# Moving the grad loads to another queue, storing dx in whole tiles and taking two softmax products to the vector engine, in a window-attention backward kernel

## The chip, the cores and the metric

The kernel runs on one core of a Trainium2 chip. The core has a matrix engine (PE; its weight loads are shown apart as PEld), a vector engine (DVE), a scalar engine (ACT), a general engine (POOL) and a synchronisation engine (SP) that computes nothing. SP, ACT and POOL can each issue memory transfers (DMAs) on a queue of their own; 16 transfer engines carry out what all queues hold. Each engine takes its instructions in order and waits on semaphores. Matrix results land in PSUM, eight banks of 128 rows by 512 floats; ACT and DVE copy them from there to the on-chip memory SBUF (128 rows, too).

The metric is the device time of one execution in microseconds (us), the median of several runs. Before the change it is 1978.06 us, the median of three (1970.09, 1978.06, 1981.67).

## The reference

Forward and backward pass of attention in 8 x 8 windows of an image of 256 x 256 pixels with 384 channels, in bf16. The kernel returns the output and the three gradients.

```python
xw = (windows of x)                          # 1024 windows, 64 pixels, C = 384
q, k, v = split(xw @ wqkv)
p = softmax(q @ k.T * C ** -0.5)
o = p @ v @ wo
# and jax.vjp of it with grad_out: gradients of x (out_1), wqkv (out_2) and wo (out_3)
```

## The kernel before

The image is cut into 128 groups of eight windows ("n", `NQ`): four tiles t of two windows each, so that a tile has 128 rows, 64 for each window (w = 0 and 1), and 384 columns. The weights are multiplied together ahead (`A_sb`, `B_sb` and their transposes). One call of `step(n)` (L352) handles group n, and prepares the next ones in its gaps: the projections of group A = n + 3, the softmax of group S = n + 2, transposes of group n + 4, loads of group n + 5.

The order on each engine is as written (`manual_schedule`, L440); waits are put in where two instructions touch the same data, and a transfer from POOL's queue also waits for the transfer eight before it on that queue. Buffers turn round by group number: X 13 groups, DO (the incoming gradient) 5, XT 3, DOT, YHT, YH, OS and DXS 2 each.

In a step, in the order of PE:

- `md` (L198): 48 small products of TT and X, which I use as the mark where a step starts (PS<-TT,X), copied to MD by DVE and ACT.
- a third of the weight-gradient sums of an earlier set of groups (`Block`, L280), in banks 3 and 4; DVE adds the banks to ACC (`add`, L306). Only in steps 0 to 2 there is none waiting (the branch `early`).
- `attn2` (L259), twice: products of the softmax with X, DO and YH; copied to VW.
- `dxs` (L268): the rest of dx into PSUM banks 5 to 7, where `attn` has begun to sum it (`DXB`, L249). Tile t lies at columns 384 t from there on. So bank 5 holds tiles 0 and 1 alone, bank 6 both pairs, bank 7 tiles 2 and 3. `dxs_ev` (L273) has ACT copy a pair of tiles (h = 0, then 1) to DXS, and POOL store it.
- `scores(S)` (L137) into bank 4; `chain0`, `chain2` and `chain3` (L152 to L171) are the softmax of S and its gradient: maximum and difference on DVE (SS), exponential on ACT (PEX), and from there DVE to L169; the last two products (UM and PB, L170 and L171) on POOL.
- `proj(A, 0)` (L119): products of A_sb and XT into banks 0 to 2, copied to YHT by ACT; `outs` (L211): products of B_sb and MD into banks 5 and 6, then 0 and 1, copied to OS by ACT, stored by POOL (`outs_st`, L218); `proj(A, 1)`: of BT_sb and DOT, into banks 7, 2, 4 and 3, copied to YHT by ACT and, the last quarter, by DVE.

The turning transfers are SP's. Each turns a 128 x 1536 bf16 array: X to XT and DO to DOT (`turn_in`, L110) and the two halves of YHT to YH (`turn_yh`, L115). SP's order in step n is: XT of n + 4, DOT of n + 4, the four loads of DO of n + 5 (`load_do`, L106; before L397), two turns YH of S. A turn to YH must have read YHT before `proj` of two groups later is copied into the same buffer.

POOL's order in step n is: loads of X of n + 5 (`load_x`, L102), stores of dx for h = 0 and then h = 1, UM and PB, stores of the output. In PSUM the two windows of a tile of dx stand with their halves exchanged (`attn`, o against r); the store puts that right: for each tile two stores of 64 rows, each from the other half of DXS.

Of the kernel before, what the change touches and what calls it, by code (L numbers as in the profile page):

```python
# [9 lines left out]
ALU = mybir.AluOpType  # L10
# [6 lines left out]
def kernel(  # L17
# [12 lines left out]
    _, H, W, C = x.shape  # L30
# [5 lines left out]
    NQ = (H // 16) * NQC  # L36
# [15 lines left out]
    PE, DVE, ACT, POOL, SP = nc.tensor, nc.vector, nc.scalar, nc.gpsimd, nc.sync  # L52
# [4 lines left out]
    PSF = PS[:].rearrange("p b c -> p (b c)")  # L57
# [12 lines left out]
    DXS = sb.tile([P, 2, 4, C], BF16, name="DXS")  # L70
    SS = sb.tile([P, 4, 64], F32, name="SS")
    PEX = sb.tile([P, 4, 64], F32, name="PEX")
    TM = sb.tile([P, 4, 64], F32, name="TM")
    UM = sb.tile([P, 4, 64], F32, name="UM")
# [13 lines left out]
    def ev(eng, out, in_):  # L88
        if eng is ACT:
            ACT.copy(out=out, in_=in_)  # L90
        else:
            DVE.tensor_copy(out=out, in_=in_)  # L92

    def img(ap, n, t):
        r0, c0 = 16 * (n // NQC), 32 * (n % NQC) + 8 * t
        return ap[0, r0:r0 + 16, c0:c0 + 8, :]

    def bcast(col):
        return ST[:, col, :].unsqueeze(2).to_broadcast([P, 4, 64])


    def load_x(q, n):  # L102
        for t in range(4):
            q.dma_start(out=X[:, (n % NX) * 4 + t, :], in_=img(x, n, t))  # L104

    def load_do(q, n):  # L106
        for t in range(4):
            q.dma_start(out=DO[:, (n % ND) * 4 + t, :], in_=img(grad_out, n, t))

    def turn_in(n, a):  # L110
        src = (X[:, (n % NX) * 4:(n % NX) * 4 + 4, :] if a == 0 else DO[:, (n % ND) * 4:(n % ND) * 4 + 4, :])
        SP.dma_start_transpose(out=XT[:, n % NXT, :, :] if a == 0 else DOT[:, n % NDT, :, :],
                               in_=src.rearrange("p t c -> p (t c)"))
# [5 lines left out]
    def proj(n, a, banks, engs):  # L119
        wgt = A_sb if a == 0 else BT_sb  # L120
        src = (XT[:, n % NXT] if a == 0 else DOT[:, n % NDT]).rearrange("p (t m) k -> p m t k", m=CK)
        i = 0
        for mo in range(CK):
            for t0, t1 in ((0, 4),) if mo < CK - 1 or len(banks) == CK else ((0, 2), (2, 4)):
                o = PS[:, banks[i], 0:P * (t1 - t0)]
                for m in range(CK):
                    mm(o.rearrange("p (t k) -> p t k", k=P), wgt[:, m, mo * P:(mo + 1) * P], src[:, m, t0:t1, :],
                       m == 0, m == CK - 1)
                ev(engs[i], YHT[:, n % NYH, a, mo, P * t0:P * t1], o)
                i += 1  # L130

    def stack(n, a, m0, m1):

        dst = HYS[:, 4 * m0:4 * m1, 0::3, :] if a == 0 else HYS[:, 4 * m0:4 * m1, 1:3, :]
        DVE.tensor_copy(out=dst, in_=YHT[:, n % NYH, a, m0:m1, :].rearrange("p m (t w k) -> p (m t) w k", w=2, k=64))
# [11 lines left out]
    HALF = (slice(0, 64), slice(64, 128))  # L147

    def sd(r, w):
        return PS[HALF[r], 4, w * 256:w * 256 + 256].rearrange("p (t k) -> p t k", t=4)  # L150
# [11 lines left out]
    def chain3(n):  # L162
        pb = PB[:, n % 2]
        DVE.tensor_reduce(out=ST[:, 1, :], in_=PEX[:], axis=AX.X, op=ALU.add)
        DVE.reciprocal(out=ST[:, 2, :], in_=ST[:, 1, :])
        DVE.tensor_tensor(out=pb[:, 1], in0=PEX[:], in1=bcast(2), op=ALU.mult)  # L166
        for w in range(2):
            DVE.tensor_tensor(out=TM[HALF[w]], in0=sd(1 - w, w), in1=pb[HALF[w], 1], op=ALU.mult)  # L168
        DVE.tensor_reduce(out=ST[:, 3, :], in_=TM[:], axis=AX.X, op=ALU.add)  # L169
        POOL.tensor_tensor(out=UM[:], in0=pb[:, 1], in1=bcast(3), op=ALU.mult)  # L170
        POOL.tensor_tensor(out=pb[:, 0], in0=TM[:], in1=UM[:], op=ALU.subtract)  # L171

    def turn_p(n):
        bb = PS[:, 7, 256:512].bitcast(BF16)
        for t in range(4):
            for a in range(2):
                for w in range(2):
                    r = slice(64 * w, 64 * w + 64)
                    o = t * P + a * 64
                    PE.transpose(bb[r, o:o + 64], PB[r, n % 2, a, t, :], ident[r, r])  # L180
        DVE.tensor_copy(out=TT[:, n % 2, :, :, :].rearrange("p t a k -> p (t a k)"), in_=bb)
# [16 lines left out]
    def md(n):  # L198
        for m in reversed(range(CK)):
            for t in range(4):  # L200
                for hh in range(2):
                    for w in range(2):
                        r = slice(64 * w, 64 * w + 64)
                        mm(PS[64 * hh:64 * hh + 64, MB[m][w], t * P:t * P + P],
                           X[r, (n % NX) * 4 + t, m * P + hh * 64:m * P + hh * 64 + 64],
                           TT[r, n % 2, t, :, :], True, True)
            for w in range(2):
                dst = MD[:, m, :, 1:3, :] if w == 0 else MD[:, m, :, 0::3, :]
                ev(DVE if (w == 0) == (m > 0) else ACT, dst, PS[:, MB[m][w], :].rearrange("p (t a k) -> p t a k", t=4, a=2))
# [39 lines left out]
    DXB = 5 * 512  # L249

    def attn_vw(n, t, f):

        attn(n, t, 0, f, DXB + t * C)
        attn(n, t, 1, f + C, DXB + t * C)

    def vw_ev(n, t, f, eng):
        ev(eng, VW[:, (n % NVW) * 4 + t, :, :].rearrange("p a c -> p (a c)"), PSF[:, f:f + 2 * C])
# [13 lines left out]
                lambda c0, c1: AT_sb[:, m, c0:c1], False, m == CK - 1)  # L271

    def dxs_ev(n, h, eng):  # L273
        ev(eng, DXS[:, n % 2, 2 * h:2 * h + 2, :].rearrange("p a c -> p (a c)"),
           PSF[:, DXB + 2 * h * C:DXB + 2 * h * C + 2 * C])
        for t in (2 * h, 2 * h + 1):
            for w in range(2):
                POOL.dma_start(out=img(out_1, n, t)[8 * w:8 * w + 8], in_=DXS[64 * (1 - w):64 * (1 - w) + 64, n % 2, t, :])  # L278

    class Block:  # L280

# [70 lines left out]
    def step(n):  # L352
        S, A = n + 2, n + 3
        doS, doA = S < NQ, A < NQ
        early = not todo
        if n + 4 < NQ:
            turn_in(n + 4, 0)
            turn_in(n + 4, 1)

        md(n)  # L360
        if early:
            if doA:
                proj(A, 0, (3, 4, 0, 5), (ACT, ACT, ACT, DVE))
            if n + 1 < NQ:
                turn_p(n + 1)
            attn_vw(n, 0, 0)
            vw_ev(n, 0, 0, ACT)
            attn_vw(n, 1, 2 * 512)
            attn_vw(n, 2, 2 * 512 + 2 * C)
            vw_ev(n, 1, 2 * 512, DVE)  # L370
            vw_ev(n, 2, 2 * 512 + 2 * C, ACT)
            attn_vw(n, 3, 0)
            vw_ev(n, 3, 0, ACT)
            if doS:
                stack(S, 0, 0, 3)
                stack(S, 1, 0, 3)
            if n + 5 < NQ:
                load_x(POOL, n + 5)
        else:
            blk = todo.pop(0)  # L380
            nb = len(blk.tiles)
            i1, i2 = (7, 15) if nb == 4 * GQ else (nb // 2, nb)
            blk.mms((3, 4), 0, i1)
            attn2(n, 0, (ACT, ACT))
            if doS:
                stack(S, 0, 0, 3)
            if n + 1 < NQ:
                turn_p(n + 1)
            if doS:
                stack(S, 1, 0, 3)  # L390
            blk.mms((3, 4), i1, i2)
            blk.add(4)
            if n + 5 < NQ:
                load_x(POOL, n + 5)
            attn2(n, 1, (ACT, DVE))
        ready(n)
        if n + 5 < NQ:  # L397
            load_do(SP, n + 5)
        if doS:
            turn_yh(S, 0)  # L400
            turn_yh(S, 1)

        dxs(n, 0)
        dxs(n, 1)
        if not early:
            if doS:
                scores(S)
                chain0(S)
            dxs_ev(n, 0, ACT)
            blk.mms((3,), i2, nb)  # L410
        dxs(n, 3)
        dxs(n, 2)
        if early:
            dxs_ev(n, 0, ACT)
            if doS:
                scores(S)
                chain0(S)
        if doS:
            chain2(S)
        dxs_ev(n, 1, ACT)  # L420
        if doS:
            chain3(S)
        if not early:
            blk.add(3)
        if doA:
            proj(A, int(early), (0, 1, 2), (ACT, ACT, ACT))
        else:
            fill(0, 1, 2)
        outs(n, 0, (5, 6), ACT)
        outs(n, 2, (4, 7) if early else (0, 1), ACT)  # L430
        outs_st(n)
        if not early and doA:
            proj(A, 1, (7, 2, 4, 3), (ACT, ACT, ACT, DVE))
        elif not doA:
            fill(7, 2, 4)
# [153 lines left out]
```

## Time and profile before

| | us |
|---|---|
| median of three runs | 1978.06 |
| lowest and highest | 1970.09, 1981.67 |
| the profiled execution | 1985.92 |
| its span on the core | 1983.8 |
| PE busy in it | 1944.9 |
| ACT busy | 1337.1 |
| POOL busy | 1317.0 |
| DVE busy | 1254.8 |

The profile is of one execution; the profiled one took 2.1 us more than its span. A line of groups reads: source line, engine, operation, what is written <- what is read, shapes, how many, then the busy time in us, the mean of one in ns, and the idle time of the engine before them with what ended it. A line of the timeline reads: start in us from the span's start, duration, engine, line, operation, how many were merged, and in brackets the idle time before it and what ended it. SP computes nothing and has no busy time; "SPq" is what its sequencer does, and the duration there is the time that an issue takes SP. "PEclk" is the share of full clock that PE was granted.

### The profile page before, as it was taken

The numbers are of one execution on the slowest core, as the hardware profiler recorded it, in microseconds if no ns is written. First come the engines' busy times: TensorE is split into PE (matmuls) and PEld (weight loads), VectorE is DVE, ScalarE is ACT, GpSimd is POOL, SyncE is SP. The second block draws the span as 40 slices with busy tenths as digits, with TensorE's granted clock in tenths as the row PEclk, the third lists the DMA queues.
The fourth block names the chain that finished last, engine by engine and source line by source line (L and its number), as shares of the span: only waits on it lengthen the run. The fifth ranks groups of instructions, "written<-read, shape, count | busy, mean of one in ns | idle before, by whom it ended". The sixth has DMA issues, their size and how long they took to land.

```text
span 1983.8 us, 78482 instructions
## 1 busy us (share of the span) xinstructions
PE 1944.9 (98%) x32789; PEld 1364.7 (69%) x32789; DVE 1254.8 (63%) x2595; ACT 1337.1 (67%) x2204; POOL 1317.0 (66%) x2315
## 2 busy tenths in 40 slices
PE   8899999999999999999999999999999999999999
PEld 5566776677667666767766776676677677666766
DVE  5665666666666666666666666666666666656664
ACT  5766766666666676667666766766776766667664
POOL 4766766666666667667667666666766766667653
PEclk9999999999999999999999999999999999999999
DMA  9999999999999999999999999999999999999992
GB/s 215 208 204 212 219 208 207 216 208 200 212 214 212 210 200 210 216 209 216 216 212 210 222 212 196 222 206 210 207 224 205 211 208 218 205 199 222 217 165 68
DMA packets 972260, 409.24 MB, mean 206 GB/s; under 512 B 855296, under 2 KB 947264, under 8 KB 971904
## 3 DMA queue, kind: packets, MB, share of 16 engines
q1 hardware_dynamic: 871632, 251.17, 83.5%
q0 software_dynamic: 98496, 151.78, 30.0%
q8 instruction: 256, 4.19, 0.9%
q10 hardware_dynamic: 1776, 1.28, 0.2%
q14 instruction: 100, 0.82, 0.1%
HBM read 101.84 MB, written 101.84 MB: 103 GB/s over the span
## 4 chain that ended last, share of the span: by engine, by line
PE 85%; DMA 10%; ACT 2%; DVE 1%; issue 1%; POOL 0%; ACTq 0%; DVEq 0%; POOLq 0%
PE PS L86 84%; DMA YH<-YHT 10%; PE PS L180 1%; ACT YHT L90 1%; DMA out_dram<-OS 0%; ACT VW L90 0%; DMA X<-in_x_dram 0%; DVE TM L168 0%; POOL out_dram L278 0%; DVE SS L156 0%; DVE ST L154 0%; ACT DXS L90 0%; ACT VW L526 0%; ACT OS L90 0%; DVE PB L166 0%
## 5 line engine op out<-in xcount | busy, mean ns | idle before, releaser
L278 POOL DMA_DIRECT2D out_dram<-DXS x1024 | 578.0, 571 | 570.5 <-ACT DXS L90 512.2
L86 PE MATMUL PS<-VW,X 64*64 64x384 bf16 (+1 forms) x8661 | 578.1, 325 | 0.0
L86 PEld LDWEIGHTS <-X 64*64 64x64 bf16 (+1 forms) x14805 | 445.2, 106 | 129.0 <-issue 33.6
L86 PEld LDWEIGHTS <-MD 128*128 128x128 bf16 x3840 | 343.1, 98 | 226.2 <-issue 43.2
L90 ACT CAST YHT<-PS 128x512 bf16<-128x512 f32 (+1 forms) x770 | 392.6, 556 | 91.9 <-DMA YH<-YHT 60.9
L90 ACT CAST VW<-PS 128x768 bf16<-128x768 f32 x384 | 294.2, 800 | 141.1 <-PE PS L86 141.0
L104 POOL DMA_DIRECT2D X<-in_x_dram x508 | 289.3, 581 | 25.3 <-PE PS L86 14.2
L220 POOL DMA_DIRECT2D out_dram<-OS x512 | 277.5, 549 | 26.5 <-issue 10.2
L86 PE MATMUL PS<-AT_sb,MD 128*128 128x384 bf16 (+2 forms) x2304 | 294.3, 273 | 0.5 <-ACT DXS L90 0.4
L92 DVE CAST YHT<-PS 128x256 bf16<-128x256 f32 (+1 forms) x129 | 55.2, 429 | 378.2 <-PE PS L86 369.0
L86 PE MATMUL PS<-B_sb,MD 128*128 128x384 bf16 x1536 | 274.1, 326 | 12.5 <-ACT YHT L90 7.8
L86 PE MATMUL PS<-XT,A_sb 128*128 128x512 bf16 (+1 forms) x1170 | 270.3, 376 | 2.6 <-DVE TM L168 1.9
L86 PE MATMUL PS<-DOT,BT_sb 128*128 128x256 bf16 (+1 forms) x1527 | 270.5, 327 | 0.0
L90 ACT CAST DXS<-PS 128x768 bf16<-128x768 f32 x256 | 204.2, 798 | 85.7 <-PE PS L86 75.9
L92 DVE CAST MD<-PS 128x512 bf16<-128x512 f32 x384 | 241.7, 683 | 10.7 <-PE PS L86 10.3
L90 ACT CAST OS<-PS 128x768 bf16<-128x768 f32 x256 | 202.9, 809 | 51.3 <-PE PS L86 45.1
L86 PEld LDWEIGHTS <-BT_sb 128*128 128x128 bf16 x1527 | 149.1, 98 | 112.5
L90 ACT CAST MD<-PS 128x512 bf16<-128x512 f32 x384 | 201.2, 602 | 28.2 <-PE PS L86 27.8
L86 PE MATMUL PS<-YH,PB 64*64 64x256 bf16 (+2 forms) x3072 | 211.7, 270 | 0.0
L160 ACT ACTIVATE PEX<-SS 128x256 f32<-128x256 f32 x128 | 53.3, 417 | 227.9 <-DVE SS L156 227.9
L86 PEld LDWEIGHTS <-PB 64*64 64x64 bf16 x6144 | 192.6, 107 | 16.4 <-issue 2.5
L86 PEld LDWEIGHTS <-A_sb 128*128 128x128 bf16 x1170 | 109.0, 98 | 110.3 <-issue 3.9
(65 smaller groups left out, 1938.6 us busy)
## 6 DMA issues: line engine op xcount, KB each, us to landing
out_dram<-DXS POOLq DMA_DIRECT2D x1024, 48.0 KB
out_dram<-OS POOLq DMA_DIRECT2D x512, 96.0 KB
X<-in_x_dram POOLq DMA_DIRECT2D x508, 96.0 KB
DO<-in_grad_out_dram SPq DMA_DIRECT2D x504, 96.0 KB, 5.1
YH<-YHT SPq DMA_TRANSPOSE x256, 8.2
XT<-X SPq DMA_TRANSPOSE x126, 7.4
DOT<-DO SPq DMA_TRANSPOSE x126, 8.2
DO<-in_grad_out_dram POOLq DMA_DIRECT2D x8, 96.0 KB
```

What stands on the lines that cost most here:

```text
L86: PE.matmul(out, lhsT=lhsT, rhs=rhs, start=start, stop=stop, skip_group_check=True)
L90: ACT.copy(out=out, in_=in_)
L92: DVE.tensor_copy(out=out, in_=in_)
L104: q.dma_start(out=X[:, (n % NX) * 4 + t, :], in_=img(x, n, t))
L160: ACT.activation(out=PEX[:], in_=SS[:], func=ACTF.Exp)
L180: PE.transpose(bb[r, o:o + 64], PB[r, n % 2, a, t, :], ident[r, r])
L220: POOL.dma_start(out=img(out_0, n, t), in_=OS[:, n % 2, t, :])
L278: POOL.dma_start(out=img(out_1, n, t)[8 * w:8 * w + 8], in_=DXS[64 * (1 - w):64 * (1 - w) + 64, n % 2, t, :])
```

## The change

The loads of DO in the loop go from SP's queue to POOL's, and later in the step: after the stores of the second pair of dx. SP then issues only turning transfers in the loop. The copy of dx from PSUM to DXS puts the halves right itself: ACT makes two copies of 64 rows x 768 columns for each pair, each from the other half of PSUM, instead of one of 128 rows. A tile of dx is then stored by one transfer of 128 rows instead of two of 64. UM and PB are computed on DVE instead of POOL. The loads ahead of the loop stay as they are. PE's instructions and their order are the same.

```diff
@@ chain3 @@
-        POOL.tensor_tensor(out=UM[:], in0=pb[:, 1], in1=bcast(3), op=ALU.mult)
-        POOL.tensor_tensor(out=pb[:, 0], in0=TM[:], in1=UM[:], op=ALU.subtract)
+        DVE.tensor_tensor(out=UM[:], in0=pb[:, 1], in1=bcast(3), op=ALU.mult)
+        DVE.tensor_tensor(out=pb[:, 0], in0=TM[:], in1=UM[:], op=ALU.subtract)
@@ dxs_ev @@
-        ev(eng, DXS[:, n % 2, 2 * h:2 * h + 2, :].rearrange("p a c -> p (a c)"),
-           PSF[:, DXB + 2 * h * C:DXB + 2 * h * C + 2 * C])
+        for w in range(2):
+            ev(eng, DXS[HALF[w], n % 2, 2 * h:2 * h + 2, :].rearrange("p a c -> p (a c)"),
+               PSF[HALF[1 - w], DXB + 2 * h * C:DXB + 2 * h * C + 2 * C])
         for t in (2 * h, 2 * h + 1):
-            for w in range(2):
-                POOL.dma_start(out=img(out_1, n, t)[8 * w:8 * w + 8], in_=DXS[64 * (1 - w):64 * (1 - w) + 64, n % 2, t, :])
+            POOL.dma_start(out=img(out_1, n, t), in_=DXS[:, n % 2, t, :])
@@ step @@
         ready(n)
-        if n + 5 < NQ:
-            load_do(SP, n + 5)
         if doS:
             turn_yh(S, 0)
             turn_yh(S, 1)
...
         dxs_ev(n, 1, ACT)
+        if n + 5 < NQ:
+            load_do(POOL, n + 5)
         if doS:
             chain3(S)
```

## The prediction

> **What bounds the kernel now.** I read the page first, then the waits, then one step in order of time, engine by engine. Part 1 of the page, and two lines of part 3 (queue, kind: packets, MB, share of 16 engines):
>
> ```profile
> PE 1944.9 (98%) x32789; PEld 1364.7 (69%) x32789; DVE 1254.8 (63%) x2595; ACT 1337.1 (67%) x2204; POOL 1317.0 (66%) x2315
> ...
> q1 hardware_dynamic: 871632, 251.17, 83.5%
> q0 software_dynamic: 98496, 151.78, 30.0%
> ```
>
> PE bounds; but a step is not always as long as PE's work. I took the start of md (PS<-TT,X) of every step from the timeline. Most steps last 14.87 us; steps 6 to 124 (119 of them) take 1801.6 us, 15.14 on average, 46 over 14.9. At 14.87 they would take 1769.8: 31.8 us are lost there. Busy time of one long step and the two after it:
>
> ```profile
> core 0: us, PE busy (x) PEld busy (x) DVE busy (x) ACT busy (x) POOL busy (x), PEclk, DMA share, GB/s
> 1226.03:1242.93 16.90, 15.04 (x259) 10.43 (x259) 9.71 (x20) 9.84 (x18) 11.55 (x22) 1.00 1.11 194
> 1242.93:1257.80 14.87, 14.87 (x259) 10.44 (x259) 9.69 (x20) 10.72 (x19) 10.06 (x19) 1.00 1.20 226
> ```
>
> The same PE work, at full clock, 2 us longer: PE waited. The waits (who <- for whom: us in total, times, longest) say for what:
>
> ```profile
> ACT YHT L90 <- DMA YH<-YHT: 60.9, 64, 3.3
> PE PS L86 <- ACT YHT L90: 18.7, 31, 1.9
> ```
>
> ACT may not overwrite YHT until the turning transfer of two steps before (turn_yh) has read it; PE then waits for ACT's copy. 31 such waits, each with some 0.25 us of restart around it in the step lengths, make about 26 of the 31.8; 1.7 more is 3.4 us at clock 0.50 from 1756.9. Why is the transfer late? SP's own instructions, in order of time, and two lines of what is on its turning line (min/median/max ns):
>
> ```profile
> 925.72 2.51 SPq L108 DMA_DIRECT2D DO<-in_grad_out_dram  x4
> 928.33 5.98 SPq L116 DMA_TRANSPOSE YH<-YHT  x2
> 934.54 3.65 SPq L112 DMA_TRANSPOSE XT<-X  x1
> 938.41 2.71 SPq L112 DMA_TRANSPOSE DOT<-DO  x1
> ...
> L112 SPq EVENT_SEMAPHORE  x749: 17/28/28, 16.7 to 1899.5; - x188
> L112 SPq DMA_TRANSPOSE XT<-X x126: 1426/2736/4576, 16.8 to 1896.4; - x126
> ```
>
> SP is never idle: its semaphore instructions last 17 to 28 ns, so what it waits for has long happened. (A turn carries one more wait itself; the YHT that is read at 943.80 was written before 926.8, so its 2.5 us aren't that.) By medians: 256 x 2.74 (YH) + 126 x 2.74 (XT) + 126 x 2.90 (DOT) + 504 x 0.60 (DO) = 1712 us between 16.8 and 1899.5; short gaps and semaphores fill most of the rest. SP's period without waiting is the 15.1 us average; PE's is 14.87. So SP lags until it holds PE up: the YH turns of the step that starts at 926.30 go out at 943.80, 17.5 us late, land 8 us later, and ACT, wanting YHT at 951.1, starts at 951.92. The lag jumps from 9 to 17 us at the three extra woT turns after step 4 and stays at 16 to 19. At the end, where no loads are left, it shrinks to 14.1, 10.3 and 4.5 us, and the steps are exactly 14.87: without SP's lag PE's 14.87 is the floor.
>
> [...] The trace agrees that they share (83.5% + 30.0% is over one), and the saved time is SP's 4 x 0.6 us; this is the ground of rival B. [...] two VW copies in a row start 0.70 apart. [...]
>
> **The change, part by part.** Rows used (busy, mean ns):
>
> ```profile
> L278 POOL DMA_DIRECT2D out_dram<-DXS x1024 | 578.0, 571 | 570.5 <-ACT DXS L90 512.2
> L90 ACT CAST DXS<-PS 128x768 bf16<-128x768 f32 x256 | 204.2, 798 | 85.7 <-PE PS L86 75.9
> ...
> L171 POOL TENSOR_TENSOR PB<-TM,UM 128x256 bf16<-128x256 f32 x128 | 93.2, 728 | 10.0
> L166 DVE TENSOR_TENSOR PB<-PEX,ST 128x256 bf16<-128x256 f32 x128 | 54.3, 424 | 4.4
> ```
>
> Part 1, loads off SP: 4 x (0.60 + 0.05) = 2.6 us of 15.1 less per step. SP needs to win only 15.14 - 14.87 = 0.27. Its turns take 1.4 us at best and 2.7 in the middle, so the transfer engines push back, and how much of the 2.6 is real is not shown. Bounds: 0, if the moved bytes hold up the turns as before; 2.6, if only issue counts; the end of the run, with X and DO both gone, shows 10.3 - 14.1 = 3.8 per step. I take 1 to 2.6: any of it removes the lag within some tens of steps and absorbs the jump at woT. Gain 30.1 (31.8 less the clock dip), of which I leave 3 for isolated late transfers: -27.
>
> Part 2, POOL's queue per step: X 4, dx stores 8 -> 4, DO +4, out stores 4: still 16 issues of 0.55 to 0.58, and UM and PB (0.63 + 0.73) gone: 1.35 us less. In order: after the second pair of dx stores (their wait for ACT now ends about 952.0) DO goes out at 953.2 to 955.5, the out stores at 955.5 instead of 955.0 (nobody waits for them), X after them. Before, this step's DO was issued by SP as late as 956.1. POOL shows no landing times; bounds are SP's 2.8 to 7.0, I take 6: landed by 961.5, 5.5 us into the next step. The DOT turn and the two YH turns queue behind it on SP: The DOT turn's issue ends at 8.4 then, and YH goes out at 8.4 and 11.1 instead of 17.5 and 20; the first is needed at 25.7, that is 17.5 with 8.2 for landing. Some 9 us of room, so 0.
>
> Part 3, dx in two 64-row passes: ACT gets 256 more of 798 ns, 0.70 back to back. No 64-row ACT row is in the trace; DVE's 64x256 and 128x256 rows both take 422, so rows are free: I take 0.70 (bounds 0.4, if rows counted, to 1.0). First pair: follows at 947.97, ends 948.7, inside the 1.78 us in which ACT waits for DVE's SS. Second pair, ACT and PE in order of time:
>
> ```profile
> 950.31 0.80 ACT L90 CAST DXS<-PS 128x768 bf16<-128x768 f32 x1
> 951.92 1.56 ACT L90 CAST YHT<-PS 128x512 bf16<-128x512 f32 x3 [0.81 <-DMA YH<-YHT]
> ...
> 952.05 2.11 PE L86 MATMUL PS<-B_sb,MD 128*128 128x384 bf16 x12
> ```
>
> It ends at 951.82. The 12 products start 0.16 apart; the first three write bank 5, which holds the first pair alone; the fourth, at 952.54, is the first to need the second pair: 0.7 us of room. YHT then starts at 951.8, while this very step had it at 951.92, after 0.81 us of waiting, and lasted 14.87. So the pass costs nothing where YHT is not late as well. Without that cover it costs 0.70 a pass: in steps 126 and 127 (PE waits 0.40 for DXS already) +1, in the first three steps (PE waits 0.71 for DXS, then 0.75 for DVE, which absorbs it) +1; bounds 0 and 4 together.
>
> Part 4, UM and PB on DVE: 2 x 0.42 after L169's end at 952.70. The ACC addition ends at 954.0 instead of 953.16; its bank is rewritten by the last products of proj near 955.6; DVE sat idle 2.99 us there. PB is ready at 953.6 instead of 955.07. 0, and one wait of 1.0 (PE for POOL's PB, step 6) goes, counted above.
>
> Sum against the profiled execution's own 1985.9: -27 + 2 - 1.7 (the dip, taken as chance) = 1959. Its median run, 1978.06, lost 7.9 us less; the floor is PE's and the same for all, so I don't scale: 1959, -1.0%. From no change a measurement of this kernel tells about 0.5%: 1968.2 to 1988.
>
> **Rivals.** B, the engines are the limit and not SP's issue: q1's turns wait behind the same bytes on q0, SP's period stays at 15.0 to 15.1, and ACT's extra passes hide in its wait for YH: 1968 to 1982. For it: turns far over their 1.4 us minimum, DMA busy in tenths of 9 throughout. Against: the load's packets leave the turns' own queue, and 0.27 of 2.6 is enough.
>
> C, slower: the 64-row pass is dearer than a 128-row one, and the second pair holds bank 6. From 950.31 to 952.54 there is room for two passes of 1.1 us; beyond that PE stalls, and 0.15 us a step undo the gain (19/122). At 1.3 us a pass the pair ends at 952.9: 0.36 + 0.25 of restart, x 122 = +75: about 2034. Against: 422 for both row counts on DVE.
>
> D, POOL delivers DO over 9 us late, since it waits for ACT before it: the YH turns are late again, by the same loop, 1970 to 1995. Against: POOL is 66% busy and gets less.
>
> **How the numbers follow.** Forecast 0.77 (1952 to 1967); B 0.12; C 0.07; D 0.04. Range 1951 to 1974: all of the first and half of B. Faster by over 0.5%: 0.78 (a little of B); within: 0.13; slower: 0.09 (C and half of D).
>
> **What would show it.** Right: SP waits (long semaphore instructions before DOT), YH goes out under 14 us into the step, ACT's wait for YH near 0, no step but the first and last far from 14.87, DXS passes near 0.8. B: turns' medians over 3 us and no SP wait. C: PE waits for ACT DXS in all steps. D: SP waits for DO and YHT still waits for YH. Wrong at its root if the steps were long for something that only coincides with the late turns.

## The result

The changed kernel takes 2228.92 us in the median of four runs (2216.74 to 2258.27); the kernel before, run beside it on the same chip, 1976.51 (1970.09 to 1981.67). The ratio is 1.126, with a 95% interval of 1.120 to 1.132: 12.6% slower. The ratio leaves out the longest of the four runs (2258.27), which lies over 1.5% above the fastest. Forecast were 1959 us, and 1951 to 1974 as the range. The profiled execution took 2230.57, its span 2228.6.

### The profile page after: what moved, and what is told of

The parts are those of the page before. It is cut to its first block, busy times and chain, and to the rows that moved or that the text cites. A ratio compares the mean times of both kernels' runs of the same rounds, so it can differ in the third digit from the quotient of the medians.

```text
span 2228.6 us, 78084 instructions
## 1 busy us (share of the span) xinstructions
PE 2007.6 (90%) x32789; PEld 1418.7 (64%) x32789; DVE 1358.4 (61%) x2851; ACT 1520.1 (68%) x2460; POOL 1092.3 (49%) x2039
## 3 DMA queue, kind: packets, MB, share of 16 engines
q8 instruction: 256, 4.19, 0.8%
## 4 chain that ended last, share of the span: by engine, by line
PE 50%; DMA 42%; ACT 4%; DVE 3%; issue 1%; ACTq 0%; DVEq 0%
PE PS L86 48%; DMA YH<-YHT 42%; ACT YHT L90 3%; PE PS L180 1%; DVE YHT L92 1%; ACT DXS L90 0%; DVE MD L92 0%; ACT VW L90 0%; DMA X<-in_x_dram 0%; DVE SS L156 0%; DVE ST L154 0%; ACT OS L90 0%; DVE HYS L135 0%; ACT VW L526 0%; ACTq L104 0%
## 5 line engine op out<-in xcount | busy, mean ns | idle before, releaser
L86 PEld LDWEIGHTS <-X 64*64 64x64 bf16 (+1 forms) x14805 | 475.9, 107 | 228.6 <-issue 150.6
L86 PE MATMUL PS<-VW,X 64*64 64x384 bf16 (+1 forms) x8661 | 597.8, 333 | 0.0
L90 ACT CAST YHT<-PS 128x512 bf16<-128x512 f32 (+1 forms) x770 | 376.4, 557 | 276.1 <-DMA YH<-YHT 241.2
L90 ACT CAST DXS<-PS 64x768 bf16<-64x768 f32 x512 | 405.9, 793 | 88.1 <-PE PS L86 77.6
L278 POOL DMA_DIRECT2D out_dram<-DXS x512 | 275.3, 542 | 363.5 <-DMA out_dram<-OS 148.7
L104 POOL DMA_DIRECT2D X<-in_x_dram x508 | 269.3, 536 | 316.0 <-DMA DO<-in_grad_out_dram 202.5
L108 POOL DMA_DIRECT2D DO<-in_grad_out_dram x500 | 274.8, 556 | 249.8 <-DMA X<-in_x_dram 98.0
L86 PE MATMUL PS<-DOT,BT_sb 128*128 128x256 bf16 (+1 forms) x1527 | 283.2, 337 | 0.0
L86 PE MATMUL PS<-TT,X 64*64 64x128 bf16 x6144 | 128.8, 220 | 117.0 <-ACT YHT L90 112.8
L86 PEld LDWEIGHTS <-PB 64*64 64x64 bf16 x6144 | 211.7, 110 | 9.3 <-issue 2.6
L90 ACT CAST OS<-PS 128x768 bf16<-128x768 f32 x256 | 202.7, 824 | 11.5 <-PE PS L86 11.2
## 6 DMA issues: line engine op xcount, KB each, us to landing
YH<-YHT SPq DMA_TRANSPOSE x256, 10.8
```

What stands on the lines that cost most here:

```text
L86: PE.matmul(out, lhsT=lhsT, rhs=rhs, start=start, stop=stop, skip_group_check=True)
L278: POOL.dma_start(out=img(out_1, n, t), in_=DXS[:, n % 2, t, :])
```

## The profile after

Part 1 of the page, and the two queues of part 3 (packets, MB, share of 16 engines):

```profile
PE 2007.6 (90%) x32789; PEld 1418.7 (64%) x32789; DVE 1358.4 (61%) x2851; ACT 1520.1 (68%) x2460; POOL 1092.3 (49%) x2039
...
q1 hardware_dynamic: 800784, 202.77, 73.6%
q0 software_dynamic: 97536, 199.88, 43.4%
```

ACT has its 256 passes more (+183 us), POOL 225 us less, as the change says; the loads of DO have gone from q1 to q0. The bytes are the same (409 MB), but they now move at 183 GB/s on average; before it was 206. PE does the same work in 90% of a longer span. In the chain that ended last PE has 50% and the turning transfer to YH 42%; before, 85% and 10%. By the starts of md, steps 6 to 124 last 17.14 us on average (before 15.14), and 102 of the 119 are over 14.95 (before 45). Two of them in a row:

```profile
core 0: us, PE busy (x) PEld busy (x) DVE busy (x) ACT busy (x) POOL busy (x), PEclk, DMA share, GB/s
998.99:1016.79 17.80, 15.28 (x257) 10.95 (x257) 10.47 (x22) 11.68 (x19) 8.91 (x17) 1.00 1.23 177
1016.79:1037.83 21.04, 16.92 (x257) 12.59 (x257) 10.48 (x22) 11.68 (x19) 7.52 (x15) 0.92 1.22 148
```

The first is 3 us too long at full clock: the lower clock of the second is not the origin. PE's busy time did grow by 63 us for the same products, at a mean granted clock of 0.979 (before 0.999); PE waits for the turns in these steps, and how much of the 63 us lengthens the run is not shown. The waits (who <- for whom: us in total, times, longest) say that the old wait has grown, and that DVE, which copies the last quarter of YHT, now has it as well:

```profile
ACT YHT L90 <- DMA YH<-YHT: 241.2, 125, 6.6
DVE YHT L92 <- DMA YH<-YHT: 231.1, 51, 9.1
...
PE PS L86 <- ACT YHT L90: 188.1, 125, 5.9
```

Before, ACT's wait for YH was 60.9 us, and PE's for ACT's YHT 18.7. SP's instructions in the same stretch (start, duration), and then its turns (min/median/max ns), first after, then before:

```profile
1010.36 3.84 SPq L112 DMA_TRANSPOSE XT<-X  x1
1014.42 5.16 SPq L112 DMA_TRANSPOSE DOT<-DO  x1
1019.69 11.57 SPq L116 DMA_TRANSPOSE YH<-YHT  x2
```

```profile
L112 SPq DMA_TRANSPOSE XT<-X x126: 1427/3700/6720, 16.9 to 2142.6; - x126
L112 SPq DMA_TRANSPOSE DOT<-DO x126: 1414/3932/7522, 23.9 to 2146.8; - x126
L116 SPq DMA_TRANSPOSE YH<-YHT x256: 1435/3917/6843, 15.0 to 2171.8; - x128
...
L112 SPq DMA_TRANSPOSE DOT<-DO x126: 1419/2896/4846, 24.0 to 1899.5; - x126
L116 SPq DMA_TRANSPOSE YH<-YHT x256: 1424/2739/5858, 14.5 to 1928.1; - x128
```

SP has nothing left but turns, and is as busy as ever: most follow the last within some 0.2 us (DOT waits longer in 18 of 93 steps between 250 and 1850 us, 1.6 us on average). But the four turns of a step now hold SP for 16.0 us (steps 10 to 119); before they took 11.7, and 2.5 went to the loads. So a step of SP is 17 us where the forecast had 12.5. A turn can also contain a wait of its own for its data or its buffer (in the trace all 508 carry one semaphore condition), but that is not what makes it long: put in order, the 256-byte packets of q1 fall to the turns in blocks of 1536, and a turn's first packet starts 4.8 us (median) after its issue begins and 0.01 us after the last packet of the turn before it (in the kernel before, 2.7 and 0.29). So the queue mostly still holds older packets, and SP waits for the transfer engines to take them. The rest of the change behaves as foreseen:

```profile
L90 ACT CAST DXS<-PS 64x768 bf16<-64x768 f32 x512 | 405.9, 793 | 88.1 <-PE PS L86 77.6
```

A pass of 64 rows costs 793 ns, and PE waits for DXS 7 times in the whole run. The question is why turns take longer when nothing but turns is on SP's queue.

## Experiments

The table has, for each kernel, the median, the ratio to the kernel before on the same chip with its interval, the mean length of steps 6 to 124 and the time that the four turns of a step hold SP (steps 10 to 119, added up from the timeline of the profiled execution). The spread between chips makes the kernel before 1976 to 1991 us, so ratios are compared, not times. For e1_loads_only no step and turns are given: its profiled execution took 2135.82 us, 1.2% more than its median.

| kernel | DO / X loaded by | dx stored in | us | ratio | step | turns |
|---|---|---|---|---|---|---|
| before | SP / POOL | halves | 1976.51 | 1 | 15.14 | 11.7 |
| after | POOL / POOL | whole tiles | 2228.92 | 1.126 (1.120 to 1.132) | 17.14 | 16.0 |
| e1_loads_only | POOL / POOL | halves | 2109.63 | 1.060 (1.053 to 1.066) | | |
| e1_loads_back | SP / POOL | whole | 1967.50 | 0.989 (0.985 to 0.994) | 14.93 | 11.2 |
| e1_sp_last | SP, behind YH / POOL | whole | 2064.91 | 1.039 (1.031 to 1.046) | 15.73 | 11.2 |
| e1_no_loads | none / POOL | whole | 1961.20 | 0.986 (0.979 to 0.993) | 14.87 | 8.3 |
| e2_loads_pool | POOL / POOL | halves | 2013.07 | 1.015 (1.009 to 1.020) | 15.37 | 10.3 |
| e2_loads_act | ACT / POOL | halves | 2254.02 | 1.134 (1.128 to 1.141) | 17.30 | 16.7 |
| e2_pause | POOL / POOL | whole | 2089.91 | 1.053 (1.046 to 1.060) | 15.97 | 13.3 |
| e2_x_on_sp | POOL / SP | whole | 1963.76 | 0.990 (0.986 to 0.994) | 14.88 | 10.8 |

**The parts of the change.** First one part alone, the part undone, the loads at another place of SP's queue, and no loads in the loop.

```diff
 e1_loads_only: the kernel before, with
-            load_do(SP, n + 5)        # ahead of the YH turns
+            load_do(POOL, n + 5)      # behind the second pair of dx stores
 e1_loads_back: the kernel after, with the reverse
 e1_sp_last: the kernel after, with
+            load_do(SP, n + 5)        # behind turn_yh(S, 1)
-            load_do(POOL, n + 5)
 e1_no_loads: the kernel after, without load_do in the loop
```

> The kernel before with one part of the change: the loads of DO go to POOL's queue, after the stores of dx. Theory L (the loads): a load in SP's own queue was a pause between turns, in which POOL's plain transfers ran alone; on POOL's queue they run beside turns all the time, and turns take SP about 3.9 us instead of 2.8. L expects the whole loss or most of it, 2180 to 2260 us. Theory S (the stores): a dx store of 128 rows holds all transfer engines where two of 64 rows held fewer, and that delays turns; the loads are innocent. S expects 1955 to 1985 us here.

> The changed kernel with the loads of DO back on SP at their old place; the 64-row copies, the whole-tile stores and the two products on DVE stay. L expects about the time before, 1965 to 1990 us (the extra ACT passes hide in ACT's waits for YH), and turns at 2.7 to 2.9 us. S expects about the changed kernel, 2150 to 2240 us.

> The changed kernel with the loads of DO on SP, but after the two YH turns of the step instead of before them. L: it matters that the load stands in SP's queue at all, so 1965 to 2000 us, near the run with the loads at their old place. If instead it is only the place in the order (a pause just ahead of the YH turns), it lies well above, over 2050 us. S expects about 2150 to 2240 us.

> The changed kernel without any load of DO in the loop (leaves out: DO of groups 5 and later is not loaded, the first five are used again). 12% of all bytes moved are gone, and SP has turns alone. If the bytes of the loads beside the turns are what costs, turns fall to 2.8 us or less and the time to PE's floor, about 1955 to 1965 us. If turns are slow because they follow one another without a pause, whatever else runs, turns stay over 3.5 us and the time over 2100 us.

e1_loads_back shows that the new copy of dx, the whole stores and the two products on DVE cost nothing, together they gain 1.1% (13 of the 119 steps over 14.95, before 45): the loss needs the move of the loads. With the loads moved alone 6.0% are lost, less than theory L expected and far more than S. A kernel of the next group, e2_loads_pool, is the same with UM and PB on DVE and loses 1.5%, so that some 4.5% are due to the products on a POOL that issues 20 transfers a step; in e1_loads_only PE waits for PB, and hardly at all for YHT:

```profile
PE PS L180 <- POOL PB L171: 134.7, 88, 4.0
```

Behind the YH turns the loads on SP cost 3.9%: their place in the queue matters, not only which queue. (Theory L had under 2000 us there.) Without the loads the turns take 8.3 us and all but one of steps 6 to 124 last 14.87, so PE's floor is where the prediction had it; but 12% of the bytes are gone there, too.

**The queue or the time between the turns.** The loads moved with the products on DVE, but dx still in halves; the same on ACT's queue, issued where ACT idles; four loads of one row (256 B) on SP at the loads' old place; and X instead of DO on SP.

```diff
 e2_loads_pool: the kernel after, with dxs_ev as in the kernel before (128 rows, stores in halves)
 e2_loads_act: e2_loads_pool, with
-            load_do(POOL, n + 5)
+            load_do(ACT, n + 5)       # t = 2, then 0 and 1, then 3, at three places
 e2_pause: the kernel after, with, ahead of turn_yh(S, 0),
+            for t in range(4):
+                SP.dma_start(out=DUM[0:1, t, :], in_=wo[t:t + 1, 0:P])
 e2_x_on_sp: the kernel after, with
-                load_x(POOL, n + 5)
+            load_x(SP, n + 5)         # ahead of turn_yh(S, 0)
```

> The kernel before with the loads of DO on POOL and UM and PB on DVE, dx stored in halves as before (the run with the loads alone lost most of its time to a new wait of PE for PB on POOL; here that is gone). Theory R (rings): with DO on POOL's queue too, all plain transfers move through one queue[...]; the transfer engines then lack time for the turns. R expects the loss here too, 2100 to 2230 us. Theory I (interplay): only whole-tile stores and loads on one queue together slow the turns; I expects 1960 to 1985 us.

> The same with the loads of DO on ACT's queue, one or two at a time in ACT's idle spots (0.6 us of ACT each). SP only turns, as in the changed kernel. R: a second queue carries plain transfers again, so turns recover and the time is 1960 to 2000 us (some loss to ACT's issues). Theory P (pause): the load was a pause between turns in SP's own queue, and without it turns crowd; P expects over 2080 us.

> The changed kernel with a pause for SP: where the loads of DO stood, SP issues four loads of one row of 256 bytes into a spare buffer (the loads of DO stay on POOL). P: the pause is what counts, so the time falls to 2050 us or less. R: the engines lack time, and a pause gives them none: 2200 to 2260 us.

> The changed kernel with X and DO exchanged: the loads of X on SP, where those of DO stood, the loads of DO on POOL. Both R and P expect about the run with the loads of DO back on SP, 1960 to 1985 us; that the place of DO itself in POOL's order is the fault (a late load holding up the DOT turn) expects over 2100 us.

e2_loads_act is as slow as the kernel after, with turns as long, so it isn't POOL's queue as such. In e2_pause SP spends 1.7 us a step on four loads (before it was 2.5) and moves 1 KB with them, and more than half of the loss goes, though less than theory P expected: what was taken from SP also served as a break between the turns. In e2_x_on_sp the loads of DO stay on POOL, at their new place, and all is well; part 1 of its page, and the DOT turn on its line:

```profile
PE 1934.5 (99%) x32789; PEld 1350.4 (69%) x32789; DVE 1357.5 (69%) x2851; ACT 1532.7 (78%) x2460; POOL 812.7 (41%) x1547
```

```profile
L112 SPq DMA_TRANSPOSE DOT<-DO x126: 1413/2298/4249, 22.8 to 1875.8; - x126
```

DOT's median is 2.3 us, against 3.9 after, with DO loaded by POOL in both. It also beats both kernels: 1.0% faster than before (0.6 to 1.4), 3 steps of 119 over 14.95.

e2_loads_pool differs from the kernel after by the copy and the stores of dx alone, and is 11% apart. It loses little, and in yet another way. Its SP and, from the same stretch, its POOL:

```profile
640.70 1.48 SPq L112 DMA_TRANSPOSE XT<-X  x1
647.16 1.68 SPq L112 DMA_TRANSPOSE DOT<-DO  x1
```

```profile
640.03 2.14 POOL L108 DMA_DIRECT2D DO<-in_grad_out_dram  x4 [1.60 <-DMA out_dram<-DXS]
```

SP stands still for 5 us ahead of DOT, and for 4.6 on average of all steps. The last load of DO is issued at 641.6 and lands 5.4 us later, at 647.0, and DOT follows at 647.16: this is rival D, in a kernel in which POOL issues 20 transfers a step and waits for earlier ones (the bracket). The turns are short there, 10.3 us. Neither theory R (2100 us and more) nor I (under 1985) has it. So loads on POOL cost 1.5% with stores in halves, whole stores (with the products on DVE) gain 1.1% with loads on SP, and both together cost 12.6%.

**Two kinds of step.** In the kernel after the turns take 8.3 us in steps 0 to 4 and 16 from step 10 on; in between lie the three woT turns behind step 4 (wo is turned into woT, which is read only after the loop). These were moved, in three kernels.

```diff
-            if n == 4:
+            if n == NQ - 2:   # e3_wot_end (after), e3_before_wot (before), e3_x_wot (e2_x_on_sp)
+            if n == 64:       # e3_wot_mid (after)
```

> The kernel after with the three woT turns issued after the turns of the last steps (step 126) instead of after step 4; nothing else moves. In the kernel after, SP's four turns take 8.3 us of a step in steps 0 to 5 and 16 us from step 10 on, and the change comes right behind the three woT turns. Theory W (two regimes: SP ahead of its work, turns short; once SP has fallen behind, turns follow each other without a pause and stay twice as long): without the push the turns stay near 8.3 to 10 us a step, steps at 14.87, 1955 to 1970 us. Theory S (the slow regime is the steady state of this order of transfers, and the first steps are fast only because they start with everything loaded): the turns slow down within some tens of steps all the same, 2150 to 2230 us.

> The kernel after with the three woT turns issued after step 64. W: steps 6 to 64 last 14.87 with turns of 8.3 to 10 us in sum, steps from 70 on last 17 with 16 us of turns; in all about 2090 us. S: the turns slow down before step 30, and nothing happens at step 64: 2150 to 2230 us.

> The kernel before with the three woT turns issued at step 126. W: its lag, 9 us before woT and 17 us after it, stays near 9 and the steps at 14.87: 1955 to 1965 us. S: the lag grows to 16 or more within some tens of steps without them, and the time stays at 1970 to 1980 us.

> The kernel after with the loads of X on SP's queue where those of DO were, those of DO on POOL's (1963.8 us before), and the three woT turns at step 126. Its steps are at 14.87 already, so only the lag of the first ten steps can go: 1957 to 1964 us by W; S expects the same or no difference, 1960 to 1966.

Neither theory had it right. e3_wot_end ran 2065.12, 2189.32, 2188.35 and 2163.66 us, e3_wot_mid 2015.77 and 2155.80: runs of the same program, 6 to 7% apart. In the profile of e3_wot_end (the run of 2065) steps 10 to 64 last 14.87 to the hundredth, with turns of 10 us, and from step 77 on 17 us with turns of 16; nothing was issued there that isn't issued in every step. In e3_wot_mid the woT turns behind step 64 are digested within four steps, and the same break comes at step 95. So the push of the woT turns is not needed for the slow steps, and without it the good ones are no lasting state either. The two stretches of e3_wot_end, and SP in a step of each:

```profile
188.90:857.10 668.20, 668.20 (x11472) 468.38 (x11467) 472.35 (x989) 532.93 (x855) 387.63 (x720) 1.00 1.13 214
1318.30:1900.00 581.70, 523.04 (x8737) 373.45 (x8737) 356.73 (x748) 398.91 (x646) 291.14 (x542) 0.99 1.23 186
```

```profile
825.01 2.68 SPq L112 DMA_TRANSPOSE XT<-X  x1
833.44 1.72 SPq L112 DMA_TRANSPOSE DOT<-DO  x1
835.27 6.41 SPq L116 DMA_TRANSPOSE YH<-YHT  x2
...
1435.83 3.97 SPq L112 DMA_TRANSPOSE XT<-X  x1
1440.02 5.30 SPq L112 DMA_TRANSPOSE DOT<-DO  x1
1445.44 7.63 SPq L116 DMA_TRANSPOSE YH<-YHT  x2
```

In the good stretch SP waits ahead of every DOT, 4.3 us on average (here from 827.69 to 833.44), in the bad one ahead of 9 in 34, 2.1 us on average. A step issues the same transfers in both: 6144 packets of turns and 512 of POOL's (those of 4 bytes left out). What differs is when: in the good one POOL's transfers move 148 to 180 GB/s in the first 6 us of a step and 37 to 67 between 7 and 14, while the turns do the reverse (37 to 120, then 112 to 172); in the bad one both are spread evenly, 59 to 126 each. The break is a drift: from step 70 to 77 XT goes out later by 1.3 us a step, from 2.4 us ahead of the step's start to 6.8 behind it, and turns of 11 become turns of 16. The kernel before has no such break; moving woT to the end there gains 0.2% (0.9978, 0.9961 to 0.9995), and on e2_x_on_sp nothing.

**The transfers by themselves.** So far it looked as if turns and plain transfers that run side by side slow each other down. This was tested with all computing left out, and then with PE busy on products of constants. The buffers are cleared between the parts, a part has 25 steps, and no computing engine paces the queues; they still wait for each other where they share a buffer. Each of the three kernels ran once.

```diff
 e4_transfers: step() is replaced by the transfers alone
+                turn_in(n, 0)
+                turn_in(n, 1)
+                turn_yh(n, 0)         # X or DO on SP: loads ahead of this line
+                turn_yh(n, 1)
+                load_x(POOL, n + 1)
+                ...                   # stores of dx, load_do(POOL, n + 1), stores of the output
 e4_fetch, e4_orders: and beside them, on PE, 259 times a step (or 76 times with 512 columns)
+                mm(PS[:, i % 8, 0:150], A_sb[:, i % 3, 0:P], w_sb[:, i % 3, 0:150], True, True)
```

> The transfers alone, all computing left out (the outputs are zeros and what lies in the buffers), in five parts of 25 steps with a clearing of the buffers between them: turns only; POOL's loads and stores only; both in the order of the kernel after; both with X on SP's queue between the DOT and the YH turns; both with DO there. Nobody paces the queues, so SP and POOL follow each other without a pause, as in the long steps. Theory M (turns and plain transfers that run side by side slow each other down): turns alone 8 to 9 us a step, POOL alone about 9 (16 issues of 0.55), the order of after 16 to 17, and with X or DO on SP 2 us or more less. Theory A (the engines' work just adds up, and the mix costs nothing): 8.3 + 196608 x 8 B at the 275 GB/s of stretches without turns = 8.3 + 5.7 = 14.0 in all three mixed orders, so that the long steps need another cause. Theory N (no interference): 9 in all.

e4_transfers: turns only, POOL's only, and the order of after (the last columns are PEclk, DMA share and GB/s):

```profile
40.00:195.00 155.00, 0.00 (x0) 0.00 (x0) 1.00 1.14 212
245.00:435.00 190.00, 0.00 (x0) 186.69 (x357) 1.00 0.65 184
500.00:763.00 263.00, 0.00 (x0) 175.22 (x331) 1.00 1.20 248
```

Turns take 7.4 us a step, POOL's transfers 8.5 (they wait for POOL's issuing), and both together 12.6 from the sixth step on (12.8 with the first), at 248 GB/s. That is less than theory A's sum of 14.0 and far from M's 16 to 17: M falls. With X or DO on SP the parts took 14.3 and 14.0 us a step, more, not less; but they are no clean comparison, since POOL, with 12 issues a step, runs ahead there and is done early (with DO on SP the last eight steps take 10 us each, those beside POOL 16). By themselves the transfers of the kernel after fit into 14.87 with 2 us to spare.

What do they meet in the kernel? PE reads its instructions from memory, 16 KB at a time: the page has 256 such packets (q8, 4.19 MB), two a step, one for every 256 products and weight loads of PE; e4_fetch and e4_orders have one for every 256, too, and with PE idle, in e4_transfers, there are none. One of them goes out at 1026.75 in the kernel after, in three stretches of 1 us from there on (last column GB/s):

```profile
1026.75:1027.75 1.00, 1.00 (x21) 0.74 (x18) 0.75 (x3) 0.99 (x2) 0.94 (x2) 1.00 2.88 159
1027.75:1028.75 1.00, 1.00 (x8) 0.61 (x7) 0.94 (x3) 0.40 (x1) 0.00 (x0) 1.00 0.15 10
1028.75:1029.75 1.00, 1.00 (x11) 0.72 (x10) 0.46 (x2) 0.47 (x2) 0.00 (x0) 1.00 0.57 43
```

In the second and third of these next to nothing moves. It is so behind the fetches in the kernels before and after and in e3_wot_end: in its good stretch the transfers fall from 236 GB/s to 98 within 1.5 us, in the bad one from 233 to 41 (means over some 90 and 70 fetches).

> The transfers alone again (all computing of the kernel left out, the outputs mean nothing), but with PE busy beside them: 259 short products a step (150 columns, as many PE instructions as in the kernel, which makes PE fetch 16 KB of instructions about twice a step) or 76 long ones of the same 16.2 us (512 columns, 0.6 fetches a step). Five parts of 25 steps: the order of after with short products; the same with long ones; X on SP with short ones; turns only with short ones; POOL's transfers only with short ones. Without PE the order of after took 12.6 us a step, the turns 7.4, POOL's 8.5. Theory F (each fetch of instructions stops the transfers for 1.2 to 2.0 us, as the dips behind the fetches in the traces of the kernels have it): 15 to 17 with short products, 13.0 to 13.8 with long ones; turns only about 8.8 to 10. Theory K (PE's reading of on-chip memory slows the transfers, however many instructions): 15 to 17 with both. Theory O (neither; the loss comes from the pacing by the computing engines): 12.6 with both.

> Transfers beside 259 short products a step again (computing left out, outputs mean nothing). Parts of 25 steps: the order of after with products of 32 rows by 32 columns of weights instead of 128 by 128 (a sixteenth of the weights' bytes and a quarter of the moving ones, the same number of instructions and fetches); then with 128 rows DO on SP between DOT and YH with whole stores of dx (e1_loads_back), the same with stores in halves (the kernel before), DO on POOL with halves (e2_loads_pool), and the order of after again. Theory F (the fetches): the 32-row part takes 16.5 to 17.5 us a step like the 128-row part before (17.1). Theory K (PE's reading): 12.9 to 14. For the orders, if these transfers and the fetches alone make the difference between the kernels: 14 to 15 with DO on SP, 16.5 to 17.5 for the order of after, with halves 14 to 16.

e4_fetch, the order of after with short products, the same with long ones, X on SP with short ones, and POOL's transfers only with short ones (PE, PEld, DVE, POOL busy, PEclk, DMA share, GB/s):

```profile
60.00:425.00 365.00, 365.00 (x5615) 364.83 (x5613) 0.00 (x0) 182.41 (x345) 1.00 1.22 186
500.00:765.00 265.00, 265.00 (x1230) 120.14 (x1229) 0.00 (x0) 173.89 (x329) 1.00 1.20 246
900.00:1140.00 240.00, 240.00 (x3696) 240.00 (x3694) 0.00 (x0) 92.33 (x176) 1.00 1.15 215
1420.00:1620.00 200.00, 200.00 (x3081) 200.00 (x3079) 0.00 (x0) 189.58 (x363) 1.00 0.63 180
```

Mean steps, by the starts of XT (the last row by POOL's loads of DO):

| transfers in the order of | PE | fetches per 15 us | step |
|---|---|---|---|
| after | idle | 0 | 12.8 |
| after | long products | 0.6 | 13.1 |
| after | products of 32 rows | 1.0 | 15.1 |
| after | short products | 1.8 | 17.1; again 16.5 |
| e2_loads_pool | short | 1.8 | 15.0 |
| before | short | 1.8 | 14.9 |
| e2_x_on_sp | short (from 886 us on, when the long products of the part before had ended, until POOL is done) | 1.8 | 14.6 |
| turns only | short | 1.8 | 8.5; with PE idle 7.6 |
| POOL's only | short | 1.8 | 8.8; with PE idle 8.5 |

With transfers and PE's instructions alone, and none of the kernel's waits for computing engines, the order of after takes 16.5 to 17.1 us a step, and the others stand as their kernels do (after 17.14, e2_loads_pool 15.37, before 15.14, e2_x_on_sp 14.88, of which none can go below PE's 14.87): theory O falls; the pacing in the kernel can make it better, as in the good stretch of e3_wot_end, but isn't needed to make it slow. The 32-row products took twice as long as meant, so that they halved the number of fetches too; F's 16.5 to 17.5 was missed, probably for that reason. But they read an eighth of what the long ones read per us (8.1 x 32 x 182 against 4.6 x 128 x 640 elements) and cost 2 us more, so it isn't PE's reading (theory K); the cost goes with the number of PE's instructions, and so of its fetches. (The part of e4_orders with DO on SP and whole stores ran beside the slow 32-row products, 14.4 us, and can't be compared.)

**How much of it the fetches are.** The packets of the traces were added up, in the 2 us from 0.5 us behind the start of each fetch, and in the rest of the time:

| | behind a fetch, GB/s | in the rest, GB/s |
|---|---|---|
| kernel before | 104 | 246 |
| kernel after | 81 | 212 |
| e4: order of after, long products | 131 | 254 |
| e4: order of after, short products | 85; again 96 | 215; again 217 |
| e4: orders of e2_loads_pool, before and e2_x_on_sp, short products | 116 to 142 | 239 to 244 |
| e4: turns only, short products | 113 | 211 |
| e4: POOL's only, short products | 188 | 175 |

Two things follow. POOL's transfers by themselves are not stopped by a fetch (188 GB/s behind it, 175 in the rest); the rate falls only in the rows where turns run (211 to 113 with turns alone). And the stalls do not tell the orders apart: by these rates a fetch takes some 1.2 us of transfer time from both kernels. Most of the 2 us a step between them is lost between the stalls, where the order of after moves less beside short products, but not beside long ones. The stalls are part of why time is short in every order; they are not shown to be why the order of after is the slow one.

**What stays open.** A fetch costs 0.9 us where only turns run (7.6 to 8.5 with one a step), which is what the stalls come to there, but in the order of after 1.9 to 2.4 beside short products (those of 32 rows among them), and 0.6 beside long ones (13.1 - 12.8 with 0.5 a step). Beside short ones that is more than the stalls themselves, so something else that goes with many instructions may have a part in it. Why the order matters so much, and why halves of dx are better than whole tiles beside loads on POOL (15.0 against 16.5), no run isolates. With halves POOL has 20 issues a step instead of 16, and a transfer waits for the one eight before it: eight half stores are 384 KB, eight whole ones 768 (48 and 96 KB each). And a half store has 8 pairs of packets (4608 and 1536 B), a whole one 16. Whether either of these is the reason is not shown. Nor is why a break between the turns helps. What made the step drift at 70 in one run and at 95 in another wasn't found.

## Why the prediction was wrong

- **What bounds the kernel now** was right as far as it went: SP late, 14.87 as PE's floor; e1_no_loads, e1_loads_back and e2_x_on_sp sit on it or close to it. It stopped at SP. That SP is never idle was taken for a lack of time to issue; but a turn holds SP while the engines still take older packets (its first one starts 4.8 us after the issue begins, before the change 2.7), as "how much of the 2.6 is real is not shown" half said. e1_loads_back shows it as well: SP issues the same loads there as before, and the steps still fall from 15.14 to 14.93 us.
- **Part 1, loads off SP, is the step that failed.** It let SP's period fall by 1 to 2.6 us, with 0 as the worst. It rose by 2.0: 2.5 us of loads went, 4.3 came back in the turns (11.7 to 16.0), the rest is short gaps. It gave no bound below nothing, since it took it that the moved bytes could hold up the turns at most as much as before. The runs show in its place that the transfers themselves need about a step's time: 14.9 us beside PE's instructions in the order of before, 16.5 to 17.1 in that of after. Order and queue are worth 2 us a step with the same bytes; what in the order makes the difference stays open.
- **Rival B** had the bound, the transfer engines and not SP's issue, and its sign was seen: medians over 3 us (3.7, 3.9 and 3.9) and no SP wait. Its price was wrong: it held the period at 15.0 to 15.1, and with that 1982 us at most. That the queues share the engines (q1 and q0 together 113% of their time before, 117% after) agrees with e2_loads_act and the kernel after, where the loads left SP's queue for ACT's and POOL's and the turns took 16.7 and 16.0 us a step instead of 11.7; the prediction weighed "the load's packets leave the turns' own queue" against it, which these two (2254 and 2229 us) show to be worth nothing.
- **Part 2, POOL's queue**: the order and the room were right where POOL had lost its products and half stores. In the good stretch of e3_wot_end DOT goes out 1.6 to 6.6 us into the step, 4.0 in the middle (5.5 forecast for the landing of DO). **Rival D** is small in the kernel after, where the waits ahead of DOT make about 0.3 us a step, but it occurs in every step of e2_loads_pool, with halves.
- **Part 3, dx in two passes**: 793 ns for 64 rows, 1.60 for two, PE's wait for DXS 7.5 us in all. **Rival C** falls. But the part was costed for ACT and PE only. Whether a whole store is another load for the transfer engines than two halves was not asked; copy and stores together are worth 11% with the loads on POOL.
- **Part 4, UM and PB on DVE**: no cost, as e1_loads_back shows of parts 2 to 4 together, and it matters the other way round: without it the moved loads cost 6.0% instead of 1.5% (e1_loads_only, e2_loads_pool).
- The sum had one term of the wrong sign: +244 us where -27 stood (2230.6 against 1985.9, both profiled executions). The other terms, +2 us in all, were a little too high: with part 1 undone the same change takes 1967.5 us, 1.1% less than the kernel before on the same chip. That this is about the gain that was forecast is chance: the forecast had it from part 1.

## What to carry to other kernels

Where the transfer engines move something in every slice (before, a DMA share of 90% or more in 39 of 40) and the DMA queue's issues take longer than at their shortest (turns of 2.7 us in the middle, 1.4 at best), treat the transfers as a second bound, and the time of an issue as theirs. Here taking issues away from the queue of the turns freed nothing, and it took away a break between them. Before moving transfers between queues, run them alone, with an engine that issues as many instructions beside them: two such runs gave the step of four orders within 4% here. A load in the queue of the turns, between them, was worth having (e1_loads_back, e2_x_on_sp), even with time on another engine free.

## What was not expected of the hardware

- Where turning transfers run, the transfers slow down for 1 to 2 us behind a fetch of 16 KB of PE's instructions, twice a step: in the mean from 233 GB/s to 41 in the bad stretch of e3_wot_end, from 236 to 98 in the good one. POOL's plain transfers alone went on unhindered (188 GB/s behind a fetch, 175 else). 259 short products a step made the same transfers take 16.5 to 17.1 us instead of 12.8, 76 long ones of the same PE time 13.1.
- One program can run in two ways for a long time: 14.87 us a step for 70 steps, 17.0 for the rest, with the same transfers in each step.
- ACT's copy of 64 rows takes as long as one of 128 (793 and 798 ns for 768 columns).
- Four loads of 256 B a step on a queue full of turns won 6% (2229 to 2090 us; ratios 1.126 and 1.053).
